# Two transposes of w2 share a two-bank tile, and w2's last columns are loaded in halves

## The chip, the cores and the metric

The kernel runs on one core of a Trainium2 chip. The metric is the device time of one execution in microseconds (us), as a median over runs. A difference of about 0.2% (0.64 us here) is what a measurement of this kernel can tell from no change.

## What is computed

The reference is a Linformer attention followed by a max-out feed-forward layer, all in fp32:

```python
k_proj = einsum('ks,bhsd->bhkd', E, k)          # 8 batches, 8 heads, 1024 positions, head size 64, 64 projected rows
v_proj = einsum('ks,bhsd->bhkd', F, v)
attn   = softmax(q @ k_proj.T / 8)              # over the 64 projected rows
x      = (attn @ v_proj) as [8192, 512]
out    = maximum(x @ w1, x @ w2) @ w_out        # w1, w2: 512 x 1024; w_out: 1024 x 512
```

## The kernel before, in words

**The algebra.** The maximum is written as relu(x (w1 - w2)) + x w2, so the kernel needs `wd_sb` = w1 - w2 (512 x 1024) for the "up" products and M = w2 w_out (512 x 512, `m_sb`) for the rest. The output of a batch is relu(x wd) w_out + x M. Many products are done by a seven-product scheme (the products `p1` to `p7` in `up_steps`, `m_steps` and `down_steps`), for which VectorE makes sums and differences of blocks.

**The stages.** The work runs over 8 batches with 2 units each. Batch 0 is the start-up: while q, k and v of batch 0 are still being loaded, TensorE projects, scores and weighs them, and between these steps the weights arrive and are prepared. From batch 1 on the up products of one unit are interleaved with the down products of the unit before. The order of the instructions on each engine is that of the program text: the list `slots` (line 1086) is written out by hand, and each slot issues its instructions on TensorE, VectorE, ScalarE and the load queue in turn.

**Around the change.** To form M, w2 is needed transposed (`w2t_sb`). TensorE transposes it in 128 x 128 blocks into PSUM, ScalarE copies the result to SBUF. Columns 0 to 255 come in two halves (`step_w2t_half`, line 556, rows of half 0 and of half 1, four blocks each); columns 256, 512 and 768 onwards come in `step_w2t` (line 569, eight transposes on line 573, one ScalarE copy of 128 x 1024 on line 581). `wd_sb` is made by VectorE: `step_wd` (line 543) for the first 256 columns and `step_wd_rows` (line 549) for the others, two subtractions each (line 552), one for each `z`, that is for rows 0 and 2, or 1 and 3, of the four blocks of rows.

Batch 0's up products are plain: `u0[fb]` and `u1[fb]` are four matmuls of 512 columns each on line 528, for one block of 128 columns of `wd_sb`, followed by a relu on ScalarE (line 537) or, for `fb` 3, on VectorE (line 539). `u0[2]`, `u0[3]` read `wd[1]` (columns 256 to 511), `u0[4]`, `u0[5]` and `u1[4]`, `u1[5]` read `wd[2]`, `u0[6]`, `u0[7]` read `wd[3]`. `S1`, `S2`, `S6` and so on are the seven products for the second half of unit 1's up product (line 779); `S6` reads the blocks that `step_tw` makes on VectorE (line 620). `M1` to `M4` are the products that form M (line 657). `sums_x` (line 732) writes sums into `w2_sb`'s first 512 columns, which are free by then.

**PSUM.** There are eight banks. Four are handed out singly (`mm_bank`). The other four are two buffers of two banks each, which `att_banks` hands out in turn; a tile is free again when its last reader is done. The attention of batch 0 uses them last in `step_at(t, 1, 0, True)` and `step_at(t, 1, 1, True)` (lines 1050 and 1053), whose results VectorE reads on line 446. Lines 1047 and 1058 ask for a tile that no instruction uses.

**The loads.** All weights and all q, k, v come through POOL's queue, as DMAs that convert fp32 to fp16. They are issued in this order: q, k and v of batch 0, then the first 256 columns of w2 and w1, then (lines 134 to 142) pairs of DMAs, one for each `z`: w2 256 to 511, w1 256 to 511, w2 512 to 1023, w1 512 to 767, w1 768 to 1023; then w_out (`wo_sb`, line 143), and the k, v, q of batch 1 and the k of batch 2. A load has one of eight counters in turn, so an issue waits for the landing of the load eight before it. The sizes in the profile are those of what is written (fp16): 128 KB for 256 columns, 256 KB for 512.

The slots around the change, before:

```python
lambda: u0[0](r0=2), lambda: u0[1](r0=2), lambda: loads(1, "v", "q", "k"),
lambda: step_w2t(256, True),
lambda: u1[0](r0=2), lambda: u1[1](r0=2), wd[1], lambda: sums_x(U[0, 1], range(4)),
u0[2], u0[3], S1, S2, lambda: step_w2t(512, True), lambda: step_w2t(768, True, True), wd[2],
u0[4], u0[5], lambda: box.pop("w2t")(), wd[3],
```

`box.pop("w2t")()` is the ScalarE copy of `step_w2t(768)`, held back to that slot.

Of the kernel before, what the change touches and what calls it, by code (L numbers as in the profile page):

```python
# [10 lines left out]
FP16 = mybir.dt.float16  # L11
# [8 lines left out]
def kernel(  # L20
# [17 lines left out]
    DF = moe_w1.shape[1]  # L38
# [26 lines left out]
    def mm_bank(dtype=FP32, n=None):  # L65
        if n is None:
            n = turn.pop(0)
            turn.append(n)
        return ps.tile([128, 512 if dtype == FP32 else 1024], dtype, tag=f"mm{n}", name="mm_ps")

    def att_banks(dtype=FP32):
        return ps.tile(
            [128, 2, 512 if dtype == FP32 else 1024], dtype, tag="att", bufs=2, name="att_ps"
        )
# [4 lines left out]
    def big(n, dtype=FP16):  # L79
        return const.tile([128, 16384 // mybir.dt.size(dtype) // 2], dtype, tag=f"big{n}", name=f"big{n}")  # L80
# [22 lines left out]
    def load_all(t, b, n, src):  # L103
        alloc(t, n)
        load(t, n, src, b, 0, H)
# [19 lines left out]
    w1_sb = big(1).rearrange("p (r f) -> p r f", r=NDC)  # L125
    w2_sb = big(2).rearrange("p (r f) -> p r f", r=NDC)
# [5 lines left out]
                in_=w.rearrange("(g p z) f -> p g z f", p=128, z=2)[:, g, :, 0:256],  # L132
            )
    for w_sb, w, f0, f1 in (
        (w2_sb, moe_w2, 256, 512), (w1_sb, moe_w1, 256, 512), (w2_sb, moe_w2, 512, DF),
        (w1_sb, moe_w1, 512, 768), (w1_sb, moe_w1, 768, DF),
    ):
        for z in range(2):
            nc.gpsimd.dma_start(
                out=w_sb.rearrange("p (g z) f -> p g z f", z=2)[:, :, z, f0:f1],  # L140
                in_=w.rearrange("(g p z) f -> p g z f", p=128, z=2)[:, :, z, f0:f1],
            )
# [376 lines left out]
    def up_slots(t, j):  # L519
        t["gt", j] = gt = gpool.tile([128, NFB, HALF], FP16, tag="gt", name="gt_sb")  # L520
        for fb in range(NFB):
            def up(fb=fb, r0=0, r1=NDC):
                if r0 == 0:
                    t["up", j, fb] = mm_bank(n=first_banks[j][fb] if r1 < NDC else fb % 2)
                h_ps = t["up", j, fb]
                order = range(NDC) if fb < 2 else (0, 2, 1, 3)
                for r in order[r0:r1]:
                    nc.tensor.matmul(  # L528
                        out=h_ps,
                        lhsT=wd_sb[:, r, fb * 128 : (fb + 1) * 128],  # L530
                        rhs=t["xt"][:, r, :, j * W : (j + 1) * W],
                        start=(r == 0), stop=(r == NDC - 1),
                    )
                if r1 < NDC:
                    return
                if fb != 3:
                    nc.scalar.activation(out=gt[:, fb, :], in_=h_ps, func=ACTF.Relu)
                else:
                    nc.vector.tensor_scalar_max(gt[:, fb, :], h_ps, 0.0)
            yield up  # L540
# [8 lines left out]
    def step_wd_rows(f0):  # L549
        for z in range(2):  # L550
            rows = lambda w: w.rearrange("p (g z) f -> p g z f", z=2)[:, :, z, f0 : f0 + 256]
            nc.vector.tensor_tensor(
                out=rows(wd_sb), in0=rows(w1_sb), in1=rows(w2_sb), op=ALU.subtract
            )

    def step_w2t_half(g, ps_t):
        for f in range(2):
            for z in range(2):
                r = 2 * g + z
                nc.tensor.transpose(  # L560
                    out=ps_t[:, (f * 2 + z) * 128 : (f * 2 + z + 1) * 128],
                    in_=w2_sb[:, r, f * 128 : (f + 1) * 128], identity=ident16,
                )
        return lambda: nc.scalar.copy(
            out=w2t_sb[:, 0:2, g * CH : (g + 1) * CH],
            in_=ps_t[:, 0 : 2 * CH].rearrange("q (f m) -> q f m", f=2),
        )

    def step_w2t(f0, att=False, hold=False):
        ps_t = att_banks(FP16)[:, 0, :] if att else mm_bank(FP16)  # L570
        for f in range(2):
            for r in range(NDC):
                nc.tensor.transpose(  # L573
                    out=ps_t[:, (f * NDC + r) * 128 : (f * NDC + r + 1) * 128],
                    in_=w2_sb[:, r, f0 + f * 128 : f0 + (f + 1) * 128],
                    identity=ident16,
                )
        fb = f0 // 128

        def copy():  # L580
            nc.scalar.copy(
                out=w2t_sb[:, fb : fb + 2, :].rearrange("q f m -> q (f m)"), in_=ps_t
            )

        if hold:
            box["w2t"] = copy
        else:
            copy()
# [17 lines left out]
    box = {}  # L606
# [102 lines left out]
    def step_tw(i, d):  # L709
        f0 = d * CH  # L710
        sub4(
            [t_w(i)[:, :, f0 : f0 + CH] for i in range(4)],
            lambda h, c: wd_sb[:, h * NX : (h + 1) * NX, c * HALF + f0 : c * HALF + f0 + CH], (i,),
        )
# [23 lines left out]
    def sums_x(u, which):  # L738
        step_s(u, x_blk, lambda i: s_x(i, u), which)
# [311 lines left out]
    u0, u1 = [*up_slots(t, 0)], [*up_slots(t, 1)]  # L1051
# [2 lines left out]
    first_banks = (0, 1), (2, 3)  # L1054
    for u in u0[0], u1[1], u0[1], u1[0]:
        u(r1=2)
    step_w2t_half(1, att_banks(FP16)[:, 0, :])()
    att_banks()


    load_all(tiles[1], 1, "k", k)
    wt = [lambda f0=f0: step_w2t(f0) for f0 in range(0, DF, 256)]
    wd = [lambda f0=f0: step_wd_rows(f0) for f0 in range(0, DF, 256)]
    f = lambda s, *a: lambda: s(tiles[0], *a)

    def loads(b, *names):
        for n in names:
            b_ = b + (n == "k" and b < 2)
            if (b_, n) == (1, "q"):
                alloc(tiles[1], "q")  # L1070
                for c in (0, NC // 2):
                    nc.gpsimd.dma_start(
                        out=tiles[1]["q"][:, :, c : c + NC // 2],
                        in_=q[1].rearrange("h (p c) d -> p h c d", c=NC)[:, :, c : c + NC // 2],
                    )
            elif (b_, n) == (2, "q"):
                alloc(tiles[2], "q")
                for h in (0, H // 2):
                    load(tiles[2], "q", q, 2, h, h + H // 2)
            elif b_ < B:  # L1080
                load_all(tiles[b_], b_, n, {"k": k, "v": v, "q": q}[n])

    open_box(0)
    S1, S2, S6, S5, S7, S3, S4 = up_steps(U[0, 1], (1,))
    M1, M2, M6, M5, M7, M3, M4, M_add = m_steps()
    slots = [
        lambda: u0[0](r0=2), lambda: u0[1](r0=2), lambda: loads(1, "v", "q", "k"),
        lambda: step_w2t(256, True),
        lambda: u1[0](r0=2), lambda: u1[1](r0=2), wd[1], lambda: sums_x(U[0, 1], range(4)),
        u0[2], u0[3], S1, S2, lambda: step_w2t(512, True), lambda: step_w2t(768, True, True), wd[2],  # L1090
        u0[4], u0[5], lambda: box.pop("w2t")(), wd[3],
        lambda: [step_tw(i, 1) for i in range(2)] and None, lambda: U[0, 1]["c0"](),
        lambda: [step_tw(i, 1) for i in range(2, 4)] and None,
        u1[4], u1[5], S6, S5, u0[6], u0[7], S7,
# [319 lines left out]
```

## Time and profile before

| | |
|---|---|
| time, median of 3 runs | 319.65 us (319.51 to 319.77) |
| the profiled execution's own time | 319.38 us |
| its span, first to last instruction | 317.5 us |
| TensorE (PE) busy | 311.8 us, 98% of the span |
| VectorE (DVE) busy | 245.1 us, 77% |
| ScalarE (ACT) busy | 207.1 us, 65% |
| GpSimd (POOL) busy | 39.9 us, 13% |
| granted TensorE clock | 1.0 |

In the profile's rows PE is the matmul side of TensorE and PEld its weight load, which runs ahead of the matmuls; L573 is line 573 of the kernel. A row of the timeline has the start, the duration, the engine, the line, the operation, the tiles written and read, the count, and in brackets how long the engine had been idle before it and what ended that. A matmul's duration is longer than the distance to the next, since matmuls are pipelined. The chain of work that ended last lists, in order of time, which instructions the end of the span hangs on.

### The profile page before, as it was taken

The numbers are of one execution on the slowest core, as the hardware profiler recorded it, in microseconds if no ns is written. First come the engines' busy times: TensorE is split into PE (matmuls) and PEld (weight loads), VectorE is DVE, ScalarE is ACT, GpSimd is POOL, SyncE is SP. The second block draws the span as 40 slices with busy tenths as digits, with TensorE's granted clock in tenths as the row PEclk, the third lists the DMA queues.
The fourth block names the chain that finished last, engine by engine and source line by source line (L and its number), as shares of the span: only waits on it lengthen the run. The fifth ranks groups of instructions, "written<-read, shape, count | busy, mean of one in ns | idle before, by whom it ended". The sixth has DMA issues, their size and how long they took to land.

```text
span 317.5 us, 9309 instructions
## 1 busy us (share of the span) xinstructions
PE 311.8 (98%) x3902; PEld 254.9 (80%) x3902; DVE 245.1 (77%) x474; ACT 207.1 (65%) x376; POOL 39.9 (13%) x63
## 2 busy tenths in 40 slices
PE   7999999999999999999999999999999999999996
PEld 3655688788887888788887888788887888888885
DVE  3368997977969696996969696997969696969883
ACT  2487843767776778477776777576776777765541
POOL 8259002002000400003000300003000100000000
PEclk9999999999999999999999999999999999999999
DMA  7999999999988799997999699997999331313134
GB/s 188 206 200 193 208 206 202 208 171 165 176 161 191 133 197 245 233 189 116 225 242 245 122 197 246 219 167 126 222 223 215 81 101 36 103 34 102 35 102 136
DMA packets 76685, 53.72 MB, mean 169 GB/s; under 512 B 29664, under 2 KB 76128, under 8 KB 76640
## 3 DMA queue, kind: packets, MB, share of 16 engines
q0 software_dynamic: 30688, 28.05, 56.5%
q1 hardware_dynamic: 45664, 24.85, 31.7%
q8 instruction: 31, 0.51, 0.6%
q10 hardware_dynamic: 288, 0.20, 0.2%
q14 instruction: 14, 0.11, 0.1%
HBM read 57.15 MB, written 16.78 MB: 233 GB/s over the span
## 4 chain that ended last, share of the span: by engine, by line
PE 92%; DMA 5%; POOL 2%; issue 0%; DVE 0%; POOLq 0%
PE mm_ps L887 47%; PE mm_ps L779 28%; DMA v_sb<-in_v_dram 5%; PE mm_ps L528 3%; PE att_ps L355 3%; PE mm_ps L197 3%; PE mm_ps L343 3%; PE att_ps L239 1%; PE att_ps L657 1%; PE mm_ps L657 1%; POOL v_sb L108 1%; DMA out_dram<-o_sb 1%; PE mm_ps L313 1%; POOL k_sb L108 0%; PE att_ps L573 0%; POOL q_sb L108 0%
## 5 line engine op out<-in xcount | busy, mean ns | idle before, releaser
L749 ACT COPY p_sb<-mm_ps 128x512 f32<-128x512 f32 x180 | 102.3, 592 | 47.9 <-PE mm_ps L779 27.8
L887 PEld LDWEIGHTS <-big 128*128 128x128 f16 x768 | 73.5, 98 | 11.8 <-issue 3.6
L887 PE MATMUL mm_ps<-T_sb,big 128*128 128x256 f16 x576 | 76.9, 273 | 0.0
L794 DVE TENSOR_TENSOR gt_sb<-mm_ps,p_sb 128x512 f16<-128x512 f32 x58 | 39.9, 688 | 42.8 <-PE mm_ps L779 41.4
L779 PE MATMUL mm_ps<-big,big 128*128 128x256 f16 x348 | 52.0, 273 | 0.0
L779 PEld LDWEIGHTS <-big 128*128 128x128 f16 x464 | 45.4, 98 | 5.7
L887 PE MATMUL mm_ps<-wo_sb,gt_sb 128*128 128x256 f16 x256 | 42.6, 273 | 0.0
L887 PEld LDWEIGHTS <-gt_sb 128*128 128x128 f16 x376 | 35.7, 98 | 6.7 <-issue 2.7
L472 ACT ACTIVATE ex_sb<-mm_ps 128x512 f16<-128x512 f32 x50 | 27.2, 596 | 18.1 <-PE mm_ps L343 12.3
L779 PEld LDWEIGHTS <-wd_sb 128*128 128x128 f16 x348 | 34.0, 98 | 4.2
L779 PE MATMUL mm_ps<-xt_sb,wd_sb 128*128 128x256 f16 x232 | 33.8, 272 | 0.0
L502 DVE TENSOR_TENSOR xt_sb<-att_ps,ld_sb 128x1024 f16<-128x1024 f32 x26 | 31.7, 1219 | 0.2
L887 PE MATMUL mm_ps<-m_sb,xt_sb 128*128 128x256 f16 x128 | 24.4, 273 | 0.0
L918 DVE TENSOR_TENSOR o_sb<-mm_ps,p_sb 128x512 f32<-128x512 f32 x32 | 21.9, 683 | 2.9 <-ACT p_sb L947 2.0
L797 DVE TENSOR_SCALAR gt_sb<-gt_sb 128x512 f16<-128x512 f16 (+1 forms) x62 | 21.9, 353 | 2.1
L305 POOL COPY junk<-qt_sb 1x1 f16<-1x1 f16 x6 | 1.2, 203 | 174.5 <-DMA qt_sb<-q_sb 174.5
L732 DVE TENSOR_TENSOR big<-gt_sb 128x1024 f16<-128x1024 f16 x32 | 21.8, 683 | 0.0
L887 PE MATMUL mm_ps<-wo_sb,big 128*128 128x256 f16 x128 | 21.5, 273 | 0.0
L856 ACT ACTIVATE gt_sb<-mm_ps 128x512 f16<-128x512 f32 x29 | 17.4, 601 | 5.7 <-PE mm_ps L779 5.7
L887 PE MATMUL mm_ps<-T_sb,gt_sb 128*128 128x256 f16 x120 | 20.3, 273 | 0.0
L794 DVE TENSOR_TENSOR gt_sb<-p_sb 128x512 f16<-128x512 f32 x29 | 19.8, 682 | 0.6 <-ACT p_sb L749 0.6
L887 PEld LDWEIGHTS <-xt_sb 128*128 128x128 f16 x188 | 18.3, 98 | 2.3 <-issue 0.2
(128 smaller groups left out, 433.1 us busy)
## 6 DMA issues: line engine op xcount, KB each, us to landing
out_dram<-o_sb SPq DMA_DIRECT2D x62, 256.0 KB
k_sb<-in_k_dram POOLq DMA_DIRECT2D x7, 1024.0 KB, 10.2
v_sb<-in_v_dram POOLq DMA_DIRECT2D x7, 1024.0 KB, 17.0
q_sb<-in_q_dram POOLq DMA_DIRECT2D x5, 1024.0 KB, 23.6
q_sb<-in_q_dram POOLq DMA_DIRECT2D x6, 512.0 KB, 16.6
big<-in_moe_w_dram POOLq DMA_DIRECT2D x12, 128.0 KB, 6.5
v_sb<-in_v_dram POOLq DMA_DIRECT2D x4, 256.0 KB, 13.5
wo_sb<-in_moe_w_out_dram POOLq DMA_DIRECT2D x1, 1024.0 KB, 10.3
```

What stands on the lines that cost most here:

```text
L197: nc.tensor.matmul(out=kv_ps[r * KP : (r + 1) * KP, h * D : (h + nh) * D], lhsT=eft[i][:, c, :], rhs=t[w][:, h0 + h : h0 + h + nh, c, :], ...
L343: nc.tensor.matmul(out=banks[e][pos : pos + z, h * W : (h + 1) * W], lhsT=kpt_of(t, head, o)[:, s : s + z], rhs=t["qt"][o * D : (o + 1) * ...
L472: nc.scalar.activation(out=t["ex", g, j][:, e, :], in_=banks[e], func=ACTF.Exp, scale=scale)
L502: nc.vector.tensor_tensor(out=x_out(t, g, j).rearrange("q z o n -> q o z n"), in0=at_ps.rearrange("q o (z n) -> q o z n", z=2), in1=ld[:, ...
L732: nc.vector.tensor_tensor(out=S(i), in0=S(0) if x is None else x, in1=y(), op=op)
L749: copy(out=x, in_=bank)
L779: nc.tensor.matmul(out=bank[:, m * W : (m + 1) * W], lhsT=w_[:, n_, (2 * d + m) * 128 : (2 * d + m + 1) * 128], rhs=a[:, n_, :], start=(n ...
L794: nc.vector.tensor_tensor(out=c_blk(j, c), in0=two(x), in1=two(y), op=ALU.add)
L797: nc.vector.tensor_scalar_max(ap, ap, 0.0)
L856: nc.scalar.activation(out=out, in_=in_, func=ACTF.Relu)
L887: nc.tensor.matmul(out=bank[i][:, 0:CH] if two_banks else bank[:, i * CH : (i + 1) * CH], lhsT=a(c)[:, i * 128 : (i + 1) * 128], rhs=w_(c) ...
L918: nc.vector.tensor_tensor(out=o_sb, in0=two(x), in1=two(y), op=ALU.add)
```

## The change

Three edits, all in batch 0. The eight transposes of columns 256 to 511 write the second bank of the two-bank tile whose first bank the second half of columns 0 to 255 uses, so they ask for no tile of their own; the two unused requests become one fewer. The loads of w2's columns 512 to 1023 are split in two, with w1's 512 to 767 between. The transposes of columns 768 to 1023 go behind `u0[5]`, and their ScalarE copy follows at once.

```diff
-        (w2_sb, moe_w2, 256, 512), (w1_sb, moe_w1, 256, 512), (w2_sb, moe_w2, 512, DF),
-        (w1_sb, moe_w1, 512, 768), (w1_sb, moe_w1, 768, DF),
+        (w2_sb, moe_w2, 256, 512), (w1_sb, moe_w1, 256, 512), (w2_sb, moe_w2, 512, 768),
+        (w1_sb, moe_w1, 512, 768), (w2_sb, moe_w2, 768, DF), (w1_sb, moe_w1, 768, DF),
...
-    def step_w2t(f0, att=False, hold=False):
-        ps_t = att_banks(FP16)[:, 0, :] if att else mm_bank(FP16)
+    def step_w2t(f0, ps_t=None, hold=False):
+        ps_t = att_banks(FP16)[:, 0, :] if ps_t is None else ps_t
...
-    step_w2t_half(1, att_banks(FP16)[:, 0, :])()
-    att_banks()
+    w2t_pair = att_banks(FP16)
+    step_w2t_half(1, w2t_pair[:, 0, :])()
...
-    wt = [lambda f0=f0: step_w2t(f0) for f0 in range(0, DF, 256)]
...
-        lambda: step_w2t(256, True),
+        lambda: step_w2t(256, w2t_pair[:, 1, :]),
...
-        u0[2], u0[3], S1, S2, lambda: step_w2t(512, True), lambda: step_w2t(768, True, True), wd[2],
-        u0[4], u0[5], lambda: box.pop("w2t")(), wd[3],
+        u0[2], u0[3], S1, S2, lambda: step_w2t(512), wd[2],
+        u0[4], u0[5], lambda: step_w2t(768, hold=True), lambda: box.pop("w2t")(), wd[3],
```

The list `wt` was called nowhere.

## The prediction

> **What bounds the kernel now.** I read the page's shares and chain first, then busy time by stage, then the chain and the timeline around the change (24 to 33 us), and last the landings of single loads. The page, then TensorE's busy time in the stages after the change's first instruction:
>
> ```profile
> PE 311.8 (98%) x3902; PEld 254.9 (80%) x3902; DVE 245.1 (77%) x474; ACT 207.1 (65%) x376; POOL 39.9 (13%) x63
> PE 92%; DMA 5%; POOL 2%; issue 0%; DVE 0%; POOLq 0%
> ...
> 26.20:48.00 21.80, 21.80 (x178) 16.07 (x180) 19.83 (x41) 14.48 (x25) 5.96 (x7) 1.00 1.28 202
> 60.00:300.00 240.00, 239.99 (x3064) 202.43 (x3051) 192.88 (x347) 167.37 (x310) 15.86 (x26) 1.00 0.85 166
> ```
>
> The second column of the last two rows is the stage's length, the third PE's busy time: 21.80 of 21.80 us and 239.99 of 240.00 us. TensorE has 92% of the chain and never stops after 26.2 us. So what TensorE gains before that shifts all that follows, if nothing else is too late for it; and nothing but TensorE can be gained. Busy says too much, as pipelined matmuls overlap, so I look for a short stall in the chain and, by engine, in the timeline:
>
> ```profile
> 25.30 0.88 PE mm_ps L528 x4
> 26.18 0.02 issue
> 26.20 0.61 PE att_ps L573 x8
> ...
> 24.77 1.28 DVE L446 TENSOR_TENSOR xt_sb<-att_ps,ld_sb 128x512 f16<-128x512 f32 x2
> 25.14 1.03 PE L528 MATMUL mm_ps<-xt_sb,wd_sb 128*128 128x512 f16 x4
> 25.34 0.59 ACT L564 COPY big<-att_ps 128x512 f16<-128x512 f16 x1 [1.83 <-PE att_ps L560]
> 26.17 0.46 PEld L573 LDWEIGHTS <-big 128*128 128x128 f16 x8 [0.50 <-issue]
> 26.20 0.61 PE L573 MATMUL att_ps<-ident,big 128*128 128x128 f16 x8
> 26.65 2.75 PE L528 MATMUL mm_ps<-xt_sb,wd_sb 128*128 128x512 f16 x12
> 29.24 1.04 PE L779 MATMUL mm_ps<-xt_sb,wd_sb 128*128 128x256 f16 x8
> ...
> L573 PEldq EVENT_SEMAPHORE  x1: 51/51/51, 26.1 to 26.1; - x1
> ...
> 23.24 1.28 DVE L446 TENSOR_TENSOR xt_sb<-att_ps,ld_sb 128x512 f16<-128x512 f32 x2
> L446 DVE TENSOR_TENSOR xt_sb<-att_ps,ld_sb x4: 681/682/684, 23.2 to 25.4; 128x512 f16<-128x512 f32 x4
> ```
>
> Twelve matmuls of 512 columns fill 26.65 to 29.24, so one takes 2.59 / 12 = 0.216 us. The four that start at 25.14 therefore leave TensorE free at 25.14 + 4 x 0.216 = 26.00. The transposes of line 573 (columns 256 to 511) start at 26.20: **a stall of 0.20 us**. The row of its sequencer (PEldq) shows the wait: an event at 26.1. VectorE's second reading of the attention tile (line 446) ends at 24.77 + 1.28 = 26.05, just before it. That tile is the one that these transposes take over, if the two requests that nothing uses take no buffer: step_at(1, 0) and step_at(1, 1) hold the two buffers, the half's transposes take the first one's, line 573 the second one's. ScalarE's copy of the half, done at 25.34 + 0.59 = 25.93, is earlier than the event and so not what ended it. I find no other stall in the stages behind it: each group starts where the matmuls before it run out.
>
> **The change, part by part.**
>
> *The shared tile: -0.20 us.* In the pair's second bank the transposes wait for the readers of step_at(1, 0) instead, done at 23.24 + 1.28 = 24.52, long before. What is late next is w2's columns 256 to 511:
>
> ```profile
> 19.11 0.71 POOL L139 DMA_DIRECT2D big<-in_moe_w_dram  x1 [1.53 <-DMA v_sb<-in_v_dram]
> 21.70 4.23 POOL L139 DMA_DIRECT2D big<-in_moe_w_dram  x6 [0.63 <-DMA v_sb<-in_v_dram]
> ...
> big<-in_moe_w_dram POOLq DMA_DIRECT2D x1, 128.0 KB, 6.8
> ...
> big<-in_moe_w_dram POOLq DMA_DIRECT2D x1, 128.0 KB, 5.1
> ...
> big<-in_moe_w_dram POOLq DMA_DIRECT2D x1, 256.0 KB, 6.3
> big<-in_moe_w_dram POOLq DMA_DIRECT2D x1, 128.0 KB, 6.2
> ```
>
> The last number of a load's row is the time from issue to landing. The second half of these columns was issued at 19.11 and landed 6.8 us later, at 25.9. TensorE is free at 26.00, so 0.1 us are left and the whole stall goes: between 0 (the load is late by 0.2) and -0.20. I take -0.20. The loads up to there are issued as before.
>
> *The halved loads: some +0.1 us on the loads behind them, nothing on TensorE.* The six issues from 21.70 are 4.23 / 6 = 0.705 us apart. The first of them, w1's last 128 KB ahead of the change (the row with 5.1), landed at 26.8. The second 256 KB piece of w2 (issued at 23.11; the row with 256.0) landed at 29.4, the first piece of w1's 512 to 767 (issued at 23.8; the row with 128.0) at 30.0. Its three followers can be seen landing in the waits of VectorE's subtractions:
>
> ```profile
> 28.90 0.42 DVE L732 TENSOR_TENSOR big<-xt_sb,big 128x512 f16<-128x512 f16 x1
> 29.44 0.69 DVE L539 TENSOR_SCALAR gt_sb<-mm_ps 128x512 f16<-128x512 f32 x1
> 30.11 1.06 PE L573 MATMUL att_ps<-ident,big 128*128 128x128 f16 x16
> 30.13 0.42 DVE L552 TENSOR_TENSOR wd_sb<-big,big 128x512 f16<-128x512 f16 x1
> 30.85 0.42 DVE L552 TENSOR_TENSOR wd_sb<-big,big 128x512 f16<-128x512 f16 x1 [0.30 <-DMA big<-in_moe_w_dram]
> 31.00 1.89 PE L528 MATMUL mm_ps<-xt_sb,wd_sb 128*128 128x512 f16 x8
> 31.33 1.29 PEld L528 LDWEIGHTS <-wd_sb 128*128 128x128 f16 x7 [0.23 <-DVE wd_sb L552]
> 31.44 0.43 DVE L552 TENSOR_TENSOR wd_sb<-big,big 128x512 f16<-128x512 f16 x1 [0.17 <-DMA big<-in_moe_w_dram]
> 32.11 0.43 DVE L552 TENSOR_TENSOR wd_sb<-big,big 128x512 f16<-128x512 f16 x1 [0.24 <-DMA big<-in_moe_w_dram]
> ```
>
> They end waits for a load at 30.85, 31.44 and 32.11, so a 128 KB piece takes (32.11 - 30.85) / 2 = 0.63 us at the least and (32.11 - 30.0) / 3 = 0.70 at the most; I take 0.67. New landings, from 26.8 on: w2 512 to 767 at 27.5 and 28.1, w1's at 28.8 and 29.5, w2's last at 30.2 and 30.8, w1's last at 31.5 and 32.2. The last was at 32.1: +0.1 us, by the two ends between 31.8 and 32.4, -0.3 to +0.3. So `wd[2]`'s input comes 1.2 us earlier, and all from `wd[3]`'s on a little later.
>
> The Trainium skill speaks against this part: its page "DMA: Bandwidth & Descriptors" (section "Anatomy of one DMA — SWDGE (gpsimd) path") gives each DMA of this queue a fixed cost of about 2 us beside its bytes. If the two more DMAs paid it one after the other, the loads behind would be 4 us late; the trace has pieces landing 0.67 us apart, so here that cost is overlapped.
>
> *Moving columns 768's transposes: nothing in TensorE's work, some slack.* The sixteen transposes of the row at 30.11 take 31.00 - 30.11 = 0.89 us, 0.056 each, so the eight that move are 0.45 us of work that goes from before `u0[4]` to behind `u0[5]`; line 573's eight from 26.00 end at 26.45. With 0.20 us gained, the transposes of column 512 start at 29.91 and end at 30.36, and `u0[4]` is due then, 0.64 us earlier than now. It needs `wd[2]`. VectorE's part: the relu of `u0[3]` (line 539) follows TensorE, 29.44 - 0.20 = 29.24, where `sums_x` (28.90 + 0.42 = 29.32 at the latest) lets it start too. The first subtraction comes 0.60 to 0.69 us behind it (two of line 446 take 1.28 where one takes 0.68; the relu itself takes 0.69), at 29.84 to 30.0, no longer tied to a load (28.8), and ends at 30.26 to 30.43. So `u0[4]` waits between 0 and 0.12 us. I take **+0.03**. The second subtraction, at most 0.43 behind, is needed only by the third matmul, 0.43 later. Without the move the second load edit would buy nothing here: today `u0[4]` starts at 31.00, behind all sixteen transposes, and even so the weight load of its third matmul waits 0.23 us for VectorE, which is hidden under the second matmul.
>
> Behind `u0[5]` (30.39 + 8 x 0.216 = 32.12) the moved transposes find their columns there since 30.8, and `u1[4]` starts at 32.57, where it started at 31.00 + 8 x 0.216 = 32.73. The copy on ScalarE comes between the relus of `u0[5]` and `u1[4]` as before. Also, `u1[4]` takes the bank of `u0[4]`, and the moved transposes give its relu 0.45 us more.
>
> *VectorE and w_out later.* `wd[3]` ends up to 0.3 us later, and with it the blocks of `step_tw`:
>
> ```profile
> 33.03 0.42 DVE L620 TENSOR_TENSOR big<-wd_sb,big 128x512 f16<-128x512 f16 x1
> 34.24 0.97 PEld L779 LDWEIGHTS <-big 128*128 128x128 f16 x8
> ...
> 26.89 0.89 POOL L143 DMA_DIRECT2D wo_sb<-in_moe_w_out_dram  x1
> 37.50 0.68 DVE L620 TENSOR_TENSOR T_sb<-wo_sb 128x1024 f16<-128x1024 f16 x1
> 37.82 0.86 PEld L657 LDWEIGHTS <-big 128*128 128x128 f16 x8
> wo_sb<-in_moe_w_out_dram POOLq DMA_DIRECT2D x1, 1024.0 KB, 10.3
> ```
>
> `S6` reads the block that is done at 33.03 + 0.42 = 33.45; its weight load is at 34.24. At worst that is 33.75 against 34.07, so 0.3 us are left. w_out was issued at 26.89 and landed 10.3 us later, at 37.2; its first use on TensorE is `M1`'s weight load at 37.82. With 0.3 us on one side and 0.17 on the other, 37.5 stands against 37.65: at worst 0.15 us are left. The two more issues on POOL (1.4 us) put its issue at 28.3, still 4 us ahead of the queue's end at 32.2. Cost nothing. The k, v and q of batch 1 queue behind it in the same way. M's later products and all of batch 1 shift with TensorE.
>
> **The sum.** -0.20 + 0.03 = -0.17 us. On the profiled execution (319.38 us) that is 319.21; the median of the runs is 0.27 above that execution, and I forecast from the median: 319.65 - 0.17 = **319.48 us**, -0.05%. Bounds of the known terms: -0.20 and 0, before what a measurement adds (the three runs are 0.26 apart). About 0.2% (0.64 us) is what a measurement of this kernel can tell from no change, so this forecast is "within 0.2%".
>
> **The rivals.**
>
> *The wait changes its owner* (for: only 0.1 us of slack at 25.9, and `u0[4]`'s due time falls on the end of VectorE's subtraction; against: both sums come out just in time). If the load is the next to be waited for, or the subtraction takes the upper end, up to all 0.20 comes back: 319.65 us, within 0.2%.
>
> *The pair is treated as one tile*, so line 573 waits for ScalarE's copy of the half: 25.93 instead of 26.05 for VectorE. The transposes came 26.20 - 26.05 = 0.15 us behind VectorE; as far behind the copy it is 26.08, 0.08 dearer than forecast: 319.56. The change then does not do what it says, and the time hardly shows it.
>
> *The loads are paced by their number, and w_out comes too late* (slower). Place: `M1`'s weight load. It decides from a delay of 37.65 - 37.2 = 0.45 us. If each further piece costs one issue of 0.705, w_out lands at 38.6 and TensorE stands 0.95 us: 319.48 + 0.95 = 320.4 us. Against it: issues run 6 us ahead of landings, and pieces of 128 KB land 0.67 apart, in proportion to 256 KB. By the Trainium skill's fixed 2 us (the page named above), paid twice, w_out would land at 41.2 and the time would be some 323 us.
>
> **How the numbers follow.** Forecast 0.65, changed owner 0.15 and one tile 0.08 (both within 0.2%), late w_out 0.08 (slower). The rest, 0.04, is for what no row shows: 0.03 faster, 0.01 within. Faster than by 0.20 us has no mechanism here. That makes 0.03 faster, 0.89 within, 0.08 slower. The range leaves out the late w_out and reaches from -0.20 to 0 with 0.15 to 0.25 for the runs' spread: 319.2 to 319.9.
>
> **What would show it.** Right: line 573's first transposes start at 26.00 with no event before them; `u0[4]` starts at 30.4, `u1[4]` near 32.57; the subtractions of `wd[2]` show no wait for a load; `M1`'s weight load is near 37.65; and the chain has TensorE alone from there. Wrong: an idle row of TensorE or its weight load before line 528 at 30.4, before `S6`, or before `M1`, with VectorE or w_out as what ended it; or a stall of TensorE after 60 us that before has not.

## The result and the profile after

The changed kernel takes **321.67 us** (median of 6 runs, 321.12 to 322.01) against 319.70 us before (6 runs on the same chip); the ratio is 1.0056, with a 95% interval of 1.0038 to 1.0074. Forecast was 319.48 us with a range to 319.9: the kernel became slower, by 2 us. Of the runs of the kernel before that stand beside `e5` to `e10` below, eight of 52 took 321.8 to 323.6 us at a granted clock of 0.989 to 0.995, which widens the intervals there, so medians are compared, which without these eight are 319.61 us (`e5` to `e8`) and 319.45 us (`e9`, `e10`).

The profiled execution took 322.01 us with a span of 320.2 (before: 319.38 and 317.5). The page of the kernel after, then TensorE's busy time in the stages that the prediction showed (length of the stage, then PE):

```profile
PE 312.6 (98%) x3902; PEld 254.9 (80%) x3902; DVE 245.4 (77%) x474; ACT 206.9 (65%) x376; POOL 41.4 (13%) x65
PE 74%; DMA 20%; POOL 2%; DVE 1%; issue 1%; ACT 0%; POOLq 0%
...
26.20:48.00 21.80, 21.16 (x170) 15.22 (x168) 18.75 (x39) 14.53 (x25) 7.38 (x9) 1.00 1.27 193
60.00:300.00 240.00, 239.06 (x3083) 201.25 (x3082) 192.44 (x344) 167.27 (x310) 15.97 (x26) 1.00 0.85 167
```

TensorE had been busy for all of 21.80 and all but 0.01 of 240.00 us. Now 0.64 us are missing in the first stage and 0.94 in the second, and the chain hangs on loads for 20% where it was 5%. The chain of waits of the kernel after, in order of time, shows which loads:

```profile
30.06 20.25 DMA v_sb<-in_v_dram
50.35 1.08 PE att_ps L239 x16
...
51.72 16.19 DMA q_sb<-in_q_dram
...
67.92 6.32 DMA qt_sb<-q_sb
...
74.38 0.41 PE mm_ps L343 x16
```

The chain no longer runs along TensorE until the scores of batch 2 at 74.38. It runs along the load queue: v of batch 1, then q of batch 2, then the DMA that transposes q.

**Around the two edits on TensorE** the forecast came true. The timeline of the kernel after, by engine:

```profile
25.22 1.03 PE L528 MATMUL mm_ps<-xt_sb,wd_sb 128*128 128x512 f16 x4
26.08 0.61 PE L573 MATMUL att_ps<-ident,big 128*128 128x128 f16 x8
...
30.46 1.90 PE L528 MATMUL mm_ps<-xt_sb,wd_sb 128*128 128x512 f16 x8
32.20 0.61 PE L573 MATMUL att_ps<-ident,big 128*128 128x128 f16 x8
...
29.99 0.75 DVE L552 TENSOR_TENSOR wd_sb<-big,big 128x512 f16<-128x512 f16 x2
31.79 0.42 DVE L552 TENSOR_TENSOR wd_sb<-big,big 128x512 f16<-128x512 f16 x1 [1.04 <-DMA big<-in_moe_w_dram]
```

The four matmuls from 25.22 leave TensorE free at 25.22 + 4 x 0.216 = 26.08, and the transposes of line 573 start then: the stall of 0.20 us is gone. `u0[4]` starts at 30.46, behind subtractions that no load holds up, and the moved transposes at 32.20.

**Where the time went.** Four places on TensorE stand where before they did not. First the kernel before (timeline, from `M1` on), then the kernel after:

```profile
37.93 1.04 PE L657 MATMUL att_ps<-wo_sb,big 128*128 128x256 f16 x8
43.61 1.04 PE L657 MATMUL att_ps<-T_sb,big 128*128 128x256 f16 x8
48.75 1.04 PE L239 MATMUL att_ps<-v_sb,eft 128*64 128x256 f16 x16
71.87 0.41 PE L343 MATMUL mm_ps<-qt_sb,kpt_sb 64*32 64x256 f16 x16
```

```profile
38.45 1.05 PE L657 MATMUL att_ps<-wo_sb,big 128*128 128x256 f16 x8 [0.43 <-DMA wo_sb<-in_moe_w_out_dram]
38.42 0.69 DVE L620 TENSOR_TENSOR T_sb<-wo_sb 128x1024 f16<-128x1024 f16 x1 [0.44 <-DMA wo_sb<-in_moe_w_out_dram]
43.86 0.58 ACT L749 COPY p_sb<-att_ps 128x512 f32<-128x512 f32 x1 [0.69 <-DVE m_sb L670]
44.50 1.03 PE L657 MATMUL att_ps<-T_sb,big 128*128 128x256 f16 x8 [0.20 <-ACT p_sb L749]
50.35 0.85 PE L239 MATMUL att_ps<-v_sb,eft 128*64 128x256 f16 x12 [0.55 <-DMA v_sb<-in_v_dram]
74.38 0.41 PE L343 MATMUL mm_ps<-qt_sb,kpt_sb 64*32 64x256 f16 x16 [0.81 <-DMA qt_sb<-q_sb]
```

| start of | before | after | later by | of that new here |
|---|---|---|---|---|
| `M1` (line 657) | 37.93 | 38.45 | 0.52 | 0.52 (a stall of 0.60; up to there TensorE was 0.08 ahead) |
| `M4` (line 657) | 43.61 | 44.50 | 0.89 | 0.37 |
| v of batch 1 (line 239) | 48.75 | 50.35 | 1.60 | 0.71 |
| scores of batch 2 (line 343) | 71.87 | 74.38 | 2.51 | 0.91 |
| end of the span | 317.5 | 320.2 | 2.6 | 0.1 |

`M1` waits for w_out. `M4` hangs on the same landing by way of VectorE: its first difference of w_out starts at 38.42 (before: 37.50), VectorE does not catch up, ScalarE waits for VectorE (`DVE m_sb L670`) before its copy at 43.86, and `M4` waits for that copy. The other two wait for loads further back in the same queue. The GpSimd rows of the kernel after (timeline) show what changed ahead of them:

```profile
26.22 2.13 POOL L139 DMA_DIRECT2D big<-in_moe_w_dram  x3 [0.32 <-DMA big<-in_moe_w_dram]
28.32 0.91 POOL L143 DMA_DIRECT2D wo_sb<-in_moe_w_out_dram  x1
```

w_out's issue, 26.89 to 27.78 before, now runs from 28.32 to 29.23, as the prediction had put it; it took that to cost nothing.

### The profile page after: what moved, and what is told of

The parts are those of the page before. It is cut to its first block, busy times and chain, and to the rows that moved or that the text cites. A ratio compares the mean times of both kernels' runs of the same rounds, so it can differ in the third digit from the quotient of the medians.

```text
span 320.2 us, 9312 instructions
## 1 busy us (share of the span) xinstructions
PE 312.6 (98%) x3902; PEld 254.9 (80%) x3902; DVE 245.4 (77%) x474; ACT 206.9 (65%) x376; POOL 41.4 (13%) x65
## 4 chain that ended last, share of the span: by engine, by line
PE 74%; DMA 20%; POOL 2%; DVE 1%; issue 1%; ACT 0%; POOLq 0%
PE mm_ps L887 41%; PE mm_ps L779 25%; DMA v_sb<-in_v_dram 10%; DMA q_sb<-in_q_dram 5%; PE mm_ps L197 3%; PE att_ps L355 3%; PE mm_ps L343 2%; DMA big<-in_moe_w_dram 2%; DMA qt_sb<-q_sb 2%; POOL k_sb L108 1%; DMA out_dram<-o_sb 1%; POOL big L139 0%; POOL q_sb L108 0%; DVE xt_sb L502 0%; DVE o_sb L918 0%
## 5 line engine op out<-in xcount | busy, mean ns | idle before, releaser
L502 DVE TENSOR_TENSOR xt_sb<-att_ps,ld_sb 128x1024 f16<-128x1024 f32 x26 | 31.7, 1218 | 0.2
```

Source lines behind the costliest of these rows:

```text
L502: nc.vector.tensor_tensor(out=x_out(t, g, j).rearrange("q z o n -> q o z n"), in0=at_ps.rearrange("q o (z n) -> q o z n", z=2), in1=ld[:, ...
```

## The experiments

**Theory A**, formed from these two traces: the two more loads make GpSimd issue w_out 1.4 us later, and the queue then has too little work ahead: the issue's **lead** over the data in front of it is too short. **Theory B**: the moved TensorE work disturbs the transfers. **Theory C**: slow packets of one execution.

For every kernel the trace has 16 landings of each load, one of each DMA engine (it does not say which engine is which). The table takes the median of the 16. Lead is from the end of w_out's issue to the landing of the last weight piece; a transfer is from the landing of the load before it to its own; stalls are gaps between matmuls beyond their usual distance. All in us. `M4`, which is not in the table, stands 0.30 to 0.37 us in the seven kernels with the late issue (`e5` and those below it).

| kernel | w_out's issue ends | last piece lands | lead | w_out's transfer | k's transfer | stall before `M1` | before batch 2's scores | time (median) |
|---|---|---|---|---|---|---|---|---|
| before | 27.78 | 31.28 | 3.50 | 5.13 | 5.07 | 0 | 0 | 319.7 |
| `e8` w1 whole between | 27.83 | 31.23 | 3.40 | 5.05 | 5.08 | 0 | 0 | 319.82 |
| `e9` shared tile alone | 27.83 | 31.21 | 3.38 | 5.08 | 5.06 | 0 | 0 | 319.46 |
| `e7` late behind w_out | 27.90 | 31.17 | 3.27 | 5.20 | 5.07 | 0 | 0 | 319.67 |
| `e2` rest alone | 28.02 | 31.25 | 3.23 | 5.10 | 5.05 | 0 | 0 | 319.79 |
| `e5` issue half as late | 28.85 | 31.13 | 2.28 | 5.20 | 5.61 | 0.17 | 0 | 320.09 |
| `e10` changed again | 29.23 | 31.32 | 2.09 | 5.52 | 5.63 | 1.01 | 1.17 | 321.58 |
| `e1` loads alone | 29.23 | 31.29 | 2.06 | 5.76 | 5.51 | 0.10 | 0.75 | 320.84 |
| after | 29.23 | 31.28 | 2.05 | 5.74 | 5.52 | 0.60 | 0.97 | 321.67 |
| `e3` halves in order | 29.31 | 31.32 | 2.01 | 5.92 | 5.44 | 0.27 | 0.90 | 321.86 |
| `e4` late issue | 29.43 | 31.41 | 1.98 | 5.95 | 5.46 | 0 | 1.22 | 321.64 |
| `e6` issue twice as late | 30.25 | 31.08 | 0.83 | 6.74 | 5.53 | 1.75 | 0.86 | 322.42 |

**`e1`: the loads alone**, on the kernel before.

```diff
-        (w2_sb, moe_w2, 256, 512), (w1_sb, moe_w1, 256, 512), (w2_sb, moe_w2, 512, DF),
-        (w1_sb, moe_w1, 512, 768), (w1_sb, moe_w1, 768, DF),
+        (w2_sb, moe_w2, 256, 512), (w1_sb, moe_w1, 256, 512), (w2_sb, moe_w2, 512, 768),
+        (w1_sb, moe_w1, 512, 768), (w2_sb, moe_w2, 768, DF), (w1_sb, moe_w1, 768, DF),
```

> The kernel before with the changed order of loads alone: w2's columns 512 to 1023 in halves with w1's 512 to 767 between; transposes and tiles as before. Theory A (two more loads ahead of w_out: GpSimd issues w_out at about 28.3 us instead of 26.9, its transfer and the ones behind it run late): w_out's last landing about 38.4, a stall of 0.4 to 0.7 us before M1, about 321.9 us, since the 0.2 us that the shared tile gains are missing here. Theory B (the moved TensorE work disturbs the transfers): as before, 319.7 us, w_out landed by 37.3. Theory C (chance of one execution): 319.7 us.

320.84 us, ratio 1.0038 (1.0025 to 1.0051). The loads alone make the kernel slower, and B falls; but by 1.2 us, not by 2.2. w_out lands as late as in the changed kernel (transfer 5.76); `M1` itself is 0.1 us later here and stands only 0.10, and v of batch 1 is not waited for.

**`e2`: the rest alone**, the changed kernel with the loads of before (the diff of `e1`, reversed).

> The changed kernel with the loads as before (w2's columns 512 to 1023 in one load for each z): the shared tile and the later last transposes alone. Theory A: w_out is issued at 26.9 again and lands at about 37.2, no stall before M1 above 0.1 us; the last transposes come after u0[5] and nothing waits for them; about 319.5 us, 0.2 below before. Theory B: 321.7 us. Theory C: 319.5 to 319.7.

319.79 us, ratio 1.0008 (0.9998 to 1.0017): w_out's transfer is 5.10 us and no stall is left from `M1` on. The 0.2 us of the shared tile don't show either; the timeline of this kernel tells why:

```profile
31.02 0.43 DVE L552 TENSOR_TENSOR wd_sb<-big,big 128x512 f16<-128x512 f16 x1 [0.28 <-DMA big<-in_moe_w_dram]
31.50 0.98 PEld L528 LDWEIGHTS <-wd_sb 128*128 128x128 f16 x6 [0.57 <-DVE wd_sb L552]
```

Without the earlier columns of w1, `wd[2]`'s second subtraction waits for its load, and `u0[4]`, which no longer has the moved transposes ahead of it, loses 0.24 us to it. So the move needs the second load edit; the prediction's term for it (+0.03) stood on w1's columns coming 1.2 us earlier.

**`e3`: the halves in the order of before**, with the rest as changed: is it the number of loads or their order?

```diff
-        ... (w2_sb, moe_w2, 512, 768), (w1_sb, moe_w1, 512, 768), (w2_sb, moe_w2, 768, DF), ...
+        ... (w2_sb, moe_w2, 512, 768), (w2_sb, moe_w2, 768, DF), (w1_sb, moe_w1, 512, 768), ...
```

> The changed kernel with w2's halves one after the other and both pieces of w1 behind them, so twelve loads of columns above 256 as in the changed kernel, but in the order of before. Theory A (the number of loads, and with it GpSimd's issue of w_out): 321.7 us and a stall before M1 of 0.4 to 0.7 us as in the changed kernel. A rival (the order, w1 between w2's halves, slows the transfers): about 319.5 us.

321.86 us, ratio 1.0061 (1.0044 to 1.0078); w_out's transfer is 5.92 us, so it is the number of loads that makes it late, not their order. This kernel has a loss of its own beside it: w1's columns 512 to 767 come late again, and the matmuls of `u0[4]` stand 0.22 and 0.25 us for `wd[2]`.

**`e4`: late issue alone.** Nothing of the change; GpSimd is only kept busy ahead of w_out's load.

```diff
+    nc.gpsimd.memset(wo_sb[:, 0:5, 0:256], 0.0)
     nc.gpsimd.dma_start(out=wo_sb, in_=moe_w_out.rearrange("(r p) f -> p r f", p=128))
```

> The kernel before with one GpSimd memset of 1280 columns on w_out's own tile ahead of w_out's load, about 1.3 to 1.5 us on GpSimd, so that w_out and all later loads are issued as late as in the changed kernel, with the ten loads of before. The memset's values are overwritten by the load. Theory A in its form 'late issue': w_out's transfer runs late as in the changed kernel, stall before M1 0.4 to 0.7 us, about 321.9 us. Theory A in its form 'the transfers of small packets themselves take longer': 319.7 to 319.9 us, w_out landed by 37.4.

321.64 us, ratio 1.0064 (1.0048 to 1.0081): **the whole loss without any part of the change.** GpSimd's rows of this kernel and, from the windows, the core's DMA traffic (last column, GB/s) while w_out's data should begin, first in this kernel, then in the one before and after:

```profile
27.06 1.19 POOL L143 MEMSET wo_sb<- 128x1280 f16 x1
28.55 0.88 POOL L144 DMA_DIRECT2D wo_sb<-in_moe_w_out_dram  x1 [0.30 <-POOL wo_sb L143]
...
31.00:32.00 1.00, 1.00 (x12) 0.61 (x10) 0.69 (x2) 0.98 (x1) 1.00 (x2) 1.00 1.08 130
```

```profile
31.00:32.00 1.00, 1.00 (x8) 0.49 (x6) 0.70 (x2) 0.77 (x1) 1.00 (x2) 1.00 1.30 213
36.50:37.50 1.00, 1.00 (x9) 0.60 (x8) 1.00 (x3) 0.73 (x2) 0.00 (x0) 1.00 1.25 208
```

```profile
31.00:32.00 1.00, 1.00 (x7) 0.41 (x6) 0.21 (x1) 1.00 (x2) 1.00 (x2) 1.00 1.03 125
36.50:37.50 1.00, 1.00 (x8) 0.68 (x7) 1.00 (x3) 0.73 (x2) 0.00 (x0) 1.00 1.06 131
```

130 and 125 GB/s where before has 213: just behind w1's last piece, where w_out's data should follow, the queue moves little. A second dip lies at 36.5, where k of batch 1 follows w_out. In this kernel's profiled execution (320.91 us, the fastest of its four) `M1` does not stand: w_out's last engine landed at 38.0, and `M1` is due at 38.2. Its loss is the 1.2 us at batch 2's scores and 0.3 at `M4`, where VectorE was late.

**`e5`, `e6`: the same with other delays**, 640 and 2560 columns instead of 1280.

```diff
+    nc.gpsimd.memset(wo_sb[:, 0:5, 0:128], 0.0)    # e5
+    nc.gpsimd.memset(wo_sb[:, 0:5, :], 0.0)        # e6
```

> The kernel before with a GpSimd memset of 640 columns on w_out's tile ahead of w_out's load, about 0.6 us; the load overwrites it. The end of w_out's issue then stands about 2.9 us ahead of the median landing of w1's last piece (before: 27.78 and 31.28, so 3.5 us; the late ones 2.0). Theory A1 (a lead that decides: between 3.5 and 2.0 us it becomes too short, and beyond that each us less costs a us): w_out's transfer from median landing to median landing stays near 5.1 us or grows by no more than 0.2; 319.7 to 320.1 us. Theory A2 (each us later costs its share, about 1.2 us on the loads for 1.5 us of delay): 0.4 to 0.5 us on the loads behind, 320.3 to 320.6 us.

> The kernel before with a GpSimd memset of 2560 columns on w_out's tile ahead of w_out's load, about 2.3 us; the load overwrites it. Lead of w_out's issue about 1.1 us. Theory A1: the 0.9 us less of lead than in the kernel that was 1.2 us late cost 0.9 us more: w_out's median landing at about 38.2, M1 stands about 1 us, all loads behind as late, 322.5 to 323.2 us. Theory A2: 0.6 to 0.8 us more than with 1.2 us, about 322.4 us. If the loss does not grow with the delay, it was not the lead: 321.6 us.

`e5`: 320.09 us against 319.61 (ratio 0.9984, 0.9951 to 1.0017, so not told apart). w_out's transfer is 5.20 as A1 has it, but that is the median of the engines: the last one lands at 38.16, where the kernels with a lead above 3 us have 37.2 to 37.5, and TensorE stands 0.17 us before `M1` and 0.36 before `M4`. k's transfer is 5.61, which A1 did not foresee. `e6`: 322.42 against 319.61 (ratio 1.0055, 1.0016 to 1.0094); w_out's transfer is 6.74, and `M1` stands 1.75 us. The windows of `e5` and `e6` (last column, GB/s), and `M1` in `e6`'s timeline, whose lines count one higher:

```profile
31.00:32.00 1.00, 1.00 (x8) 0.37 (x6) 0.70 (x2) 0.82 (x1) 1.00 (x2) 1.00 1.16 174
36.50:37.50 1.00, 1.00 (x8) 0.52 (x6) 1.00 (x3) 0.73 (x3) 0.00 (x0) 1.00 0.96 126
```

```profile
31.00:32.00 1.00, 1.00 (x8) 0.40 (x6) 0.72 (x2) 0.72 (x1) 1.00 (x3) 1.00 0.70 59
...
39.63 1.03 PE L658 MATMUL att_ps<-wo_sb,big 128*128 128x256 f16 x8 [1.58 <-DMA wo_sb<-in_moe_w_out_dram]
```

59 GB/s: with 0.83 us of lead the core's DMA traffic falls to about a quarter of before's 213 for a microsecond. Taking before's 5.13 us off w_out's median landing gives the moment at which its data in effect began: 2.44 us behind the end of its issue in `e6` (37.82 - 5.13 - 30.25), 2.80 in `e4`, 2.66 in the changed kernel, 2.48 in `e10`, 2.35 in `e5`. So **w_out's data in effect flow some 2.4 to 2.8 us after its issue ends**, and a load whose issue ends less than that ahead of the queue's end leaves a hole. It is a band, not one number, and neither A1 nor A2 describes it: w_out's transfer is longer by 0.07 us at a lead of 2.28, by 0.82 at 1.98 and by 1.61 at 0.83. In time, `e6` came out as A2 had it; A1's range began at 322.5.

The packets of w_out show more. They are of 1 KB, those of the last pieces ahead of it in `e6` of 512 bytes. The first one of w_out starts at 30.95 there, 0.70 us behind the end of the issue; but only 50 of its 1024 have started by 32.25, where the queue at its full rate starts some 50 in every quarter of a microsecond. A little of the load starts early and most of it about 2 us behind the issue. What holds the rest back stays open.

The first load of the kernel before, into an empty queue, shows a delay too, but not the same number: its issue ends at 2.10, the first packet of this queue starts at 4.59, 2.49 us later, and by the working used for w_out (256 KB, median landing at 6.85) its data in effect began 3.5 us behind the issue.

The Trainium skill (page "DMA: Bandwidth & Descriptors", section "Anatomy of one DMA — SWDGE (gpsimd) path") has the fixed cost of about 2 us that the prediction cited, and says that completion, not setup, makes most of it. The size is near the 2.4 to 2.8 us. Where it lies is not as the page has it: of the first load, 2.49 us lie between the issue and the first packet, and only 0.3 us between the end of its last packet (6.54) and its median landing; the measurement decides. Here the cost is hidden where the issue ends 3.2 us or more ahead of the end of the data before it, and it is not paid per load: two more loads cost 0.6 us on w_out's transfer, not 4.

**`e7`: the delay behind w_out**, on a tile that nothing else writes before 37.5 us.

```diff
+    nc.gpsimd.memset(T_sb[:, 0, 0:5, :], 0.0)
     load_all(tiles[1], 1, "k", k)
```

> The kernel before with a GpSimd memset of 1280 columns behind w_out's load and ahead of k's of batch 1, on a part of T_sb that is written over later: w_out is issued at 26.9 as before, k, v and q of batch 1 as late as in the changed kernel, about 1.2 us. Theory A (the lead of w_out alone: k's data are due some 7 us behind its issue): no loss, 319.6 to 319.9 us, no stall before M1 or before the scores of batch 2. A rival (the loss comes from the issues of k, v and q of batch 1 being late): 320.5 to 321.6 us.

319.67 us against 319.61 (ratio 0.9977, 0.9941 to 1.0012). k, v and q of batch 1 are issued as late as in the changed kernel (k's issue ends at 29.88), and nothing is lost: k's data are due 6.5 us behind the end of its issue, the others' later still. So it is w_out's issue alone. Its windows:

```profile
31.00:32.00 1.00, 1.00 (x9) 0.38 (x7) 0.76 (x2) 0.83 (x1) 1.00 (x2) 1.00 1.29 213
36.50:37.50 1.00, 1.00 (x7) 0.57 (x6) 1.00 (x3) 0.73 (x3) 0.00 (x0) 1.00 1.24 207
```

**`e8`: w1's columns 512 to 1023 whole between w2's halves**, with the rest as changed: halves, but ten loads.

```diff
-        (w1_sb, moe_w1, 512, 768), (w2_sb, moe_w2, 768, DF), (w1_sb, moe_w1, 768, DF),
+        (w1_sb, moe_w1, 512, DF), (w2_sb, moe_w2, 768, DF),
```

> The changed kernel with w1's columns 512 to 1023 in one load for each z between w2's halves, so ten loads of columns above 256 as before, and w2's columns 768 to 1023 last: shared tile and later transposes as changed. Theory A: the lead of w_out is back at about 3.5 us, no loss of the loads; the shared tile's 0.2 us is left unless the last transposes (due at 32.2) wait for w2's last piece, whose last engine lands at about 32.1: 319.4 to 319.7 us. A rival (halved loads cost whatever their number): 321 us or more.

319.82 us against 319.61 (ratio 1.0001, 0.9957 to 1.0044). The lead is back and so are the transfers. It ends 0.1 above the range expected: w1's piece for the second `z` now comes later, and the third matmul of `u0[4]`, due at 30.85, starts at 31.42; it loses 0.57 us waiting for `wd[2]`, more than the shared tile gains (timeline, TensorE's weight load and VectorE):

```profile
31.42 0.98 PEld L528 LDWEIGHTS <-wd_sb 128*128 128x128 f16 x6 [0.90 <-DVE wd_sb L552]
30.94 0.43 DVE L552 TENSOR_TENSOR wd_sb<-big,big 128x512 f16<-128x512 f16 x1 [0.61 <-DMA big<-in_moe_w_dram]
```

So the changed loads bought `wd[2]` its time with two issues, and the two can't both be had in this order.

**`e9`: the shared tile alone**, loads and transposes in the order of before; the one part of the change that nothing spoke against, so also the candidate to beat both kernels.

```diff
-    step_w2t_half(1, att_banks(FP16)[:, 0, :])()
-    att_banks()
+    w2t_pair = att_banks(FP16)
+    step_w2t_half(1, w2t_pair[:, 0, :])()
...
-        lambda: step_w2t(256, True),
+        lambda: step_w2t(256, w2t_pair[:, 1, :]),
```

> The kernel before with the shared tile alone: loads in the order of before, the last transposes ahead of wd[2] as before. The stall of 0.20 us ahead of the transposes at 26.1 goes. If nothing behind it takes it back: 319.4 to 319.5 us. Rival: the blocks behind come 0.2 us earlier while wd[2]'s subtractions wait for w1's columns 512 to 767 as before, so the wait appears ahead of u0[4], as it did where the last transposes were moved and the loads were not (0.24 us at 31.05): 319.6 to 319.8 us, no difference.

319.46 us against 319.45 (319.71 with all 21 runs); ratio 0.9984 (0.9961 to 1.0007). The time shows no gain. The timeline of this kernel has it at its place, and shows where it goes:

```profile
25.30 1.03 PE L528 MATMUL mm_ps<-xt_sb,wd_sb 128*128 128x512 f16 x4
26.16 0.61 PE L573 MATMUL att_ps<-ident,big 128*128 128x128 f16 x8
...
30.07 1.06 PE L573 MATMUL att_ps<-ident,big 128*128 128x128 f16 x16
30.96 3.26 PE L528 MATMUL mm_ps<-xt_sb,wd_sb 128*128 128x512 f16 x14
...
43.09 0.59 ACT L749 COPY p_sb<-att_ps 128x512 f32<-128x512 f32 x1 [0.41 <-DVE m_sb L670]
43.73 1.03 PE L657 MATMUL att_ps<-T_sb,big 128*128 128x256 f16 x8
```

25.30 + 4 x 0.216 = 26.16, so no stall there, and `u0[4]` follows its sixteen transposes at once (30.07 + 0.89 = 30.96). But the third matmul of `u0[4]` now loses 0.07 us to `wd[2]`'s second subtraction, and `M4` stands 0.09 us: ScalarE's copy ahead of it waits for VectorE. Up to `M4`, 0.16 of the 0.20 us are given back, nearly as the rival in the expectation had it, though mostly at another place. Some of the 0.09 us is the spread of executions: `e7`, without the shared tile, stands 0.07 us at `M4` too. But the kernel before had no room there. Its copy (timeline, ScalarE) was still released by TensorE:

```profile
42.93 0.59 ACT L749 COPY p_sb<-att_ps 128x512 f32<-128x512 f32 x1 [0.29 <-PE att_ps L657]
```

VectorE's addition on line 670, for which this copy waits too, ended at 42.84 there, 0.09 us ahead of the copy; in `e9` the copy also starts 0.10 us behind that addition (42.99). VectorE's work, in turn, follows the last pieces of w1, on whose landing `wd[3]` waits, and what TensorE does earlier does not move those. So by these rows a gain of TensorE alone ahead of `M4` can hardly pass it.

**`e10`: the changed kernel once more**, with no edit.

> The changed kernel once more, for the spread of its stalls. If the lead of w_out's issue decides, w_out's transfer takes 5.6 to 6.0 us again, k's of batch 1 about 5.5, and TensorE stands before M1 (0.3 to 0.7 us), in M4 (0.37) and before the scores of batch 2 (0.7 to 1.2); the 0.7 us at v of batch 1 may or may not be there, as one engine's lag made it. 321.1 to 322.1 us. If one execution's slow packets made it: 319.5 to 320 us and a transfer of 5.1 us.

321.58 us, ratio 1.0051 (1.003 to 1.0072). C falls: the late transfers come again (w_out's 5.52, a little under the range expected). The stalls are spread otherwise:

```profile
38.90 0.83 PE L657 MATMUL att_ps<-wo_sb,big 128*128 128x256 f16 x6 [0.84 <-DMA wo_sb<-in_moe_w_out_dram]
...
74.28 0.41 PE L343 MATMUL mm_ps<-qt_sb,kpt_sb 64*32 64x256 f16 x16 [1.01 <-DMA qt_sb<-q_sb]
```

`M1` stands 1.01 us, more than the 0.7 expected, the scores of batch 2 1.17, and v of batch 1 not at all. `M1` waits for the last of the 16 engines, which lands w_out 0.6 to 2.0 us behind the median in these kernels; so kernels with the same lead stand differently long there.

## Why the prediction was wrong, step by step

*The shared tile, -0.20 us:* right at its place: the stall of 0.20 us is gone in the changed kernel and in `e9`. But the sum carried it to the end of the span ("what TensorE gains before that shifts all that follows, if nothing else is too late for it"), and in `e9` VectorE was too late for it: 0.16 us were given back by `M4`. That `M4` had no room on VectorE's side was not looked for.

*The halved loads, some +0.1 us on the loads behind:* right for the pieces, at the upper end. w1's last piece has its median landing at 31.28 in both kernels, and its last engine at 32.42 instead of 32.08 (forecast: 32.2, at most 32.4).

*The moved transposes, +0.03:* right. `u0[4]` at 30.46 is the 30.39 forecast plus the 0.08 us by which that execution was later from the start (25.22 instead of 25.14). The load edit was needed for it, as `e2` shows.

*"The two more issues on POOL (1.4 us) put its issue at 28.3, still 4 us ahead of the queue's end at 32.2. Cost nothing.":* **this step failed.** The issue came at 28.32. But what counts is its end, 29.23, and the queue's end in the median, 31.28: the lead was 2.05 us, not 4. And the step took any lead above zero for enough, where the runs show 2.4 to 2.8 us to be needed: 3.2 us and more cost nothing, 2.28 already let TensorE stand. A hint stood in the trace of before: 2.49 us from the end of the first load's issue to the first packet. Taken over, it would have given 29.23 + 2.5 = 31.7 against 31.3, or w_out 0.4 us late. w_out's last landing was 38.4 where 37.5 at worst had been forecast, and `M1` stood 0.60 us. `e4` has the loss with this step alone, `e8` has the rest of the change without it.

*"The k, v and q of batch 1 queue behind it in the same way. M's later products and all of batch 1 shift with TensorE.":* the second error, and where the larger part of the loss arose. Before, k, v and q of batch 1 and k of batch 2 land 5.07, 5.07, 2.81, 2.65 and 5.06 us apart (medians 41.48, 46.55, 49.36, 52.01, 57.07): the loads follow each other without a gap, so a microsecond lost at w_out isn't made up, and reaches every load behind. TensorE's 98% made it look like the only bound, but the queue is one beside it. Of the two places behind `M4` where TensorE now stands, v of batch 1 had 1.4 us of slack before (it had landed at 47.36) and the scores of batch 2 had less. The rows of the queue that issues the transposing DMA (SPq) and of GpSimd's copy that waits for its landing, before and after:

```profile
66.08 2.48 SPq L325 DMA_TRANSPOSE qt_sb<-q_sb  x1
70.69 0.18 POOL L305 COPY junk<-qt_sb 1x1 f16<-1x1 f16 x1 [19.10 <-DMA qt_sb<-q_sb]
```

```profile
67.92 3.12 SPq L325 DMA_TRANSPOSE qt_sb<-q_sb  x1
74.30 0.18 POOL L305 COPY junk<-qt_sb 1x1 f16<-1x1 f16 x1 [21.09 <-DMA qt_sb<-q_sb]
```

Before, the transposed q was there at 70.69 and the scores started at 71.87, which leaves 1.2 us. After, q came 1.84 us later, its transpose took 6.38 us instead of 4.61, and the scores stood 0.97. The queue's lateness alone would not have done it, since TensorE came to this place 1.60 us later itself: some 0.9 us would have been left. The rest is one DMA engine. 15 of the 16 landings of the transpose were there 4.74 us after its issue (before: 4.53), the last only after 6.32. At v of batch 1 it is the same: 15 landings were there by 48.76, in time for TensorE, and the last at 50.31. Why an engine lags is open; that the late issue brings it on is shown by the runs only as far as the scores go, where all six kernels with a lead of 2.1 us or less have the lag and the six others do not.

*The rivals:* "the loads are paced by their number, and w_out comes too late" was the one that came, with a chance of 0.08. It had place and direction right (`M1`; w_out at 38.4 where it said 38.6), and its threshold of 0.45 us was passed (1.2). Its mechanism was half right: the pieces were not paced by their number, since w1's last one landed at the same median; the two issues told on w_out alone. Its price, 0.95 us, was near `M1`'s own (0.60 and 1.01), but it ended there and had nothing for `M4`, v and the scores. It was dismissed with "issues run 6 us ahead of landings", a number that has the transfer in it. The range ended at 319.9 since it left this case out.

## What to carry to other kernels

In a queue that never runs dry, look for each load at the time from the end of its issue to the end of the data ahead of it: small pieces use up an engine's issue time (0.71 us each here, against 0.67 us of data), so splitting loads eats the lead of whatever follows them. A load is there when the last of its 16 engines has landed, so look at that one and not at the median. Once the lead falls below what the queue needs (here 3.2 us was enough and 2.3 was not quite), the hole is not where the split was but at the next large load, and everything behind is late by it. A bound that is busy 98% of the time doesn't exclude a second one: before calling a transfer hidden, follow its queue to the next place where an engine waits for it with little to spare. The same goes for a gain: before carrying it to the end of the span, look for the next place where another engine is only just in time.

## What the runs showed of the hardware that was not expected

- w_out's data in effect flow 2.4 to 2.8 us after GpSimd's issue ends, in the seven kernels that issue it late; the first load of the kernel before, into an empty queue, took 3.5 us by the same working. A few of w_out's packets start much earlier (0.70 us in `e6`).
- k's transfer behind a late w_out takes 5.44 to 5.63 us instead of 5.05 to 5.08, also in `e5`, where the median of w_out itself lost 0.07 us, and not in `e7`, where k alone was issued late. The dip at 36.5 belongs to it (126 GB/s in `e5`, 207 in `e7`). Its cause stays open.
- The DMA that transposes q of batch 2 landed 4.4 to 4.8 us after its issue in the six kernels where it started by 66.8 us, and 6.1 to 6.4 in the six where it started at 67.06 or later. It is one engine that makes the difference: in all twelve, 15 of the 16 landings are there after 4.3 to 4.8 us. This makes 1.8 us of lateness into 3.6. Why was not tried.
- In the changed kernel and in `e3` one of the 16 engines landed its part of v of batch 1 at 50.3 and 50.6, 2.7 and 2.8 us behind the median, elsewhere 0.5 to 1.4. That is the stall at line 239, 0.7 us in the changed kernel and 0.6 in `e3`, which `e1`, `e4` and `e10` don't have. What held that engine up stays open.
